# Casting loads for q and k and single-head transposes in a fused attention and gMLP kernel

## The chip, the cores and the metric

The kernel runs on one core of one Trainium2 chip. The metric is the device time of one execution in microseconds (us), lower is better. Most executions of one kernel agree within about 1%. Executions over 1.5% slower than the fastest of the same kernel are left out of the means. The medians below are over all runs, and four of them hold one slow run each; without it they are 174.1 us for e5, 171.1 for e9, 170.16 for e11 and 171.15 for e12. Where a ratio with an interval is given, it is the mean time of one kernel's fast runs over the mean time of the other's fast runs of the same rounds, so it is not quite the ratio of the medians that stand beside it. The interval is the 95% interval.

Engines: PE is the matrix engine (PEld its weight loads), DVE the vector engine, ACT the scalar engine, POOL the GpSimd engine, SP the engine that only issues DMA here. `L266` in a profile line is line 266 of that kernel, so the same step has another line number in each kernel; the text says which step it is.

## The reference, cut to what matters

Attention over 4 batches, 8 heads, 768 positions and 64 dimensions, with a window of 128 and 4 sink positions; then a gated MLP whose gate mixes positions with a 768 x 768 matrix.

```python
scores = scale * q @ k.T                   # 4 x 8 heads, 768 x 768
keep = (pos_k < n_sink) | ((rel >= 0) & (rel < window))
a = softmax(where(keep, scores, -1e9))
x = (a @ v) laid out as [B, S, H * D]      # D = 64, H * D = 512

h = gelu(x @ w_in)                         # 512 -> 1024
u, v = halves of h
v_n = layernorm(v) * g_ln
v_s = einsum('ts,bsd->btd', w_sg, v_n) + b_sg[None, :, None]   # the spatial matmul
out = x + (u * v_s) @ w_out
```

## The kernel before

The kernel is a list of steps, `STEPS`, in one order; each engine executes its own steps in that order and waits, by semaphores, for the data they need. A step is named by what it does, then batch, pair of heads and so on. The names that matter here: LQ, LK, LV load; CQ, CK, CV cast to bf16; TQ, TK transpose on PE; EQ, EK copy the transposes out of PSUM; QK scores, EX exp, MK mask, SK the scores of the sink positions, AV the product with v, NR the division; XD transposes the attention result by DMA; MV and MU are the two halves of the first MLP matmul, SP the spatial matmul, GM the gating product, OU the last projection. `HOLDS` adds waits: "LQ.1.0<LWS" means that this load is issued only when LWS has landed.

```python
# ... (cut: STEPS, 60 lines; it begins)
# IDEN ZERO LC MASK LQ.0.0 LK.0.0 LQ.0.1 LK.0.1 VSK LQ.0.2 LK.0.2 LV.0.0 LQ.0.3 LK.0.3 CQ.0.0 ...
# (and around the DMA transposes of batch 1, which batch 1's MLP waits for)
# ... QK.2.0.1 AV.1.2.0 GM.0.0.2 CQ.2.3 XD.1.1 OU.0.5 ... KS.2.0 XD.1.0 EX.2.1.2 ... LV.3.0 MV.1.2 LQ.3.1 ...
HOLDS = "LQ.1.0<LWS LG<LWS"

def LQ(b, p):                                   # plain fp32 load of one pair of heads, on SP
    return nc.sync.dma_start(out=q32.new((b, p)), in_=q[b, 2 * p:2 * p + 2].rearrange("h (p t) d -> p h (t d)", p=128))

def cast(dst, src):                             # on POOL
    return nc.gpsimd.tensor_scalar(out=dst, in0=src, scalar1=1.0, scalar2=1.0, op0=ALU.mult, op1=ALU.mult)

def CQ(b, p):                                   # interleaves the two heads: [128, NT, 2, 64]
    return cast(q16.new((b, p)).rearrange("p t h d -> p h t d"),
                q32[b, p].rearrange("p h (t d) -> p h t d", d=Dh))
# ... (LK, CK alike)

def transposes(name, ring, b, p):               # six 128 x 128 transposes, two heads in each
    src = ring[b, p].rearrange("p t h d -> p t (h d)")
    mm_ring.new((name, b, p))
    ps = psb((name, b, p))
    for t in range(NT):
        nc.tensor.transpose(ps[:, t, :], src[:, t, :], iden)

def SK(b, p0):                                  # four matmuls accumulate in one 128-row result
    prs = range(HP) if b else (p0,)
    ps = mm_ring.new(("s", b, p0))
    for n, p in enumerate(prs):
        nc.tensor.matmul(ps, ks_sink[b % 2][:, 128 * p:128 * (p + 1)], qT[b, p][:, 256:768],
                         start=(n == 0), stop=(n == len(prs) - 1))

def XD(b, half):                                # transposing DMA, on SP, batches 1 to 3
    ts = slice(3 * half, 3 * half + 3)
    return nc.sync.dma_start_transpose(out=xT.get(b)[:, ts, :, :].rearrange("p t c i -> p (t c) i"),
                                       in_=x_sb[b][:, ts, :].rearrange("p t d -> p (t d)"))
# ... (cut)
```

The softmax here doesn't subtract the row's maximum and nothing guards it: scores larger than these inputs give would overflow.

Of the kernel before, what the change touches and what calls it, by code (L numbers as in the profile page):

```python
# [8 lines left out]
F32 = mybir.dt.float32  # L9
# [6 lines left out]
IDEN ZERO LC MASK LQ.0.0 LK.0.0 LQ.0.1 LK.0.1 VSK LQ.0.2 LK.0.2 LV.0.0 LQ.0.3 LK.0.3 CQ.0.0 LV.0.1 LV.0.2 TQ.0.0  # L16
CK.0.0 VSM.1 LV.0.3 EQ.0.0 TK.0.0 CQ.0.1 EK.0.0 VSM.3 TQ.0.1 CK.0.1 VSM.0 QK.0.0.2 QK.0.0.1 EX.0.0.2 KS.0.0 TK.0.1
EQ.0.1 CQ.0.2 SK.0.0 VSM.2 TQ.0.2 CK.0.2 EQ.0.2 SX.0.0 QK.0.0.0 MK.0.0.2 TK.0.2 EX.0.0.1 CV.0.0 EK.0.2 MK.0.0.1
EX.0.0.0 QK.0.2.2 KS.0.2 CQ.0.3 EX.0.2.2 MK.0.0.0 QK.0.2.0 LW.0 EK.0.1 QK.0.2.1 LW.1 EX.0.2.1 AV.0.0.0 KS.0.1 TQ.0.3
NR.0.0.0 EX.0.2.0 SK.0.1 MK.0.2.2 SK.0.2 MK.0.2.1 AV.0.0.1 SX.0.2 CK.0.3 MK.0.2.0 QK.0.1.0 SX.0.1 QK.0.1.1 CV.0.1  # L20
EX.0.1.0 NR.0.0.1 EQ.0.3 CV.0.2 EX.0.1.1 QK.0.1.2 CV.0.3 MK.0.1.0 TK.0.3 EX.0.1.2 XT.0.0 MK.0.1.1 LWS AV.0.2.1 EK.0.3
AV.0.2.0 XE.0.0 NR.0.2.1 MK.0.1.2 QK.0.3.2 QK.0.3.1 AV.0.1.0 EX.0.3.2 KS.0.3 NR.0.2.0 SK.0.3 LWO AV.0.1.1 EX.0.3.1
NR.0.1.0 QK.0.3.0 MK.0.3.2 XT.0.2 SX.0.3 NR.0.1.1 EX.0.3.0 MK.0.3.1 XT.0.1 XE.0.2 AV.0.3.1 MK.0.3.0 XE.0.1 NR.0.3.1
AV.0.3.0 NR.0.3.0 XT.0.3 XE.0.3 MV.0.2 MU.0.3 GV.0.2 LQ.1.0 LK.1.0 WT.3 WT.4 LV.1.0 WE.3 WT.5 LG WT.2 WE.4 GU.0.3
MV.0.0 WE.5 LQ.1.1 WE.2 LK.1.1 BN.0.2 LV.1.1 MV.0.1 GV.0.0 LQ.1.2 CQ.1.0 LK.1.2 RS.0.2 LV.1.2 BN.0.0 MU.0.0 LQ.1.3
GV.0.1 CK.1.0 LK.1.3 LV.1.3 Z.0.5 WT.1 RS.0.0 LQ.2.0 GU.0.0 TK.1.0 BN.0.1 LK.2.0 MU.0.1 EK.1.0 CV.1.0 Z.0.0 WE.1
TQ.1.0 WT.0 RS.0.1 Z.0.4 Z.0.1 LV.2.0 MU.0.2 WE.0 GU.0.1 EQ.1.0 CQ.1.1 GU.0.2 CK.1.1 Z.0.2 TQ.1.1 LQ.2.1 QK.1.0.2
Z.0.3 QK.1.0.0 LK.2.1 CV.1.1 EX.1.0.2 EQ.1.1 TK.1.1 SP.0.0.3 LV.2.1 CQ.1.2 SP.0.1.2 GT.0.0.3 LQ.2.2 EK.1.1 CK.1.2
GM.0.0.3 SP.0.0.1 EX.1.0.0 GT.0.1.2 MK.1.0.2 LK.2.2 GM.0.1.2 QK.1.1.0 GT.0.0.1 SP.0.1.0 CV.1.2 EX.1.1.0 MK.1.0.0
QK.1.1.1 LV.2.2 GM.0.0.1 CQ.1.3 SP.0.1.1 GT.0.1.0 EX.1.1.1 MK.1.1.0 LQ.2.3 CK.1.3 TQ.1.3 GT.0.1.1 TK.1.2 TQ.1.2  # L30
MK.1.1.1 LK.2.3 EQ.1.3 EK.1.2 TK.1.3 QK.1.0.1 EK.1.3 QK.1.1.2 EQ.1.2 SP.0.0.0 CV.1.3 EX.1.0.1 GM.0.1.1 CQ.2.0 LV.2.3
SP.0.1.3 KS.1.0 EX.1.1.2 MK.1.0.1 LQ.3.0 GT.0.0.0 QK.1.2.1 SK.1.0 GM.0.1.0 EX.1.2.1 GM.0.0.0 MK.1.1.2 GT.0.1.3
QK.1.3.1 SX.1.0 TQ.2.0 GM.0.1.3 MK.1.2.1 QK.1.3.2 EX.1.3.1 EQ.2.0 AV.1.0.0 OU.0.3 NR.1.0.0 CQ.2.1 AV.1.0.1 RA.0.3
MK.1.3.1 TQ.2.1 EX.1.3.2 NR.1.0.1 AV.1.1.1 ST.0.3 QK.1.2.2 CK.2.1 EQ.2.1 QK.1.3.0 EX.1.2.2 AV.1.1.0 OU.0.4 MK.1.3.2
NR.1.1.1 EX.1.3.0 NR.1.1.0 TK.2.1 CQ.2.2 AV.1.3.1 EK.2.1 RA.0.4 QK.1.2.0 CK.2.0 TQ.2.2 NR.1.3.1 EX.1.2.0 ST.0.4
QK.2.1.1 MK.1.2.2 LK.3.0 TK.2.0 EQ.2.2 SP.0.0.2 EX.2.1.1 CK.2.2 MK.1.2.0 EK.2.0 AV.1.2.1 GT.0.0.2 MK.2.1.1 TK.2.2
NR.1.2.1 QK.2.0.2 EK.2.2 QK.2.0.1 AV.1.2.0 GM.0.0.2 CQ.2.3 XD.1.1 OU.0.5 EX.2.0.2 MK.1.3.0 CK.2.3 NR.1.2.0 EX.2.0.1
TQ.2.3 AV.1.3.0 CV.2.2 RA.0.5 TK.2.3 QK.2.1.0 EQ.2.3 MK.2.0.1 EK.2.3 ST.0.5 QK.2.1.2 OU.0.0 EX.2.1.0 NR.1.3.0 CV.2.3
OU.0.2 KS.2.0 XD.1.0 EX.2.1.2 CV.2.1 QK.2.0.0 RA.0.0 SK.2.0 EX.2.0.0 MK.2.1.2 RA.0.2 ST.0.0 OU.0.1 MK.2.1.0 SX.2.0
ST.0.2 CV.2.0 MK.2.0.0 AV.2.1.1 MK.2.0.2 LV.3.0 MV.1.2 LQ.3.1 RA.0.1 CQ.3.0 LK.3.1 NR.2.1.1 ST.0.1 LV.3.1 CK.3.0  # L40
AV.2.0.0 GV.1.2 LQ.3.2 AV.2.1.0 NR.2.0.0 LK.3.2 MV.1.1 LV.3.2 NR.2.1.0 LQ.3.3 LK.3.3 TK.3.0 BN.1.2 LV.3.3 GV.1.1
MV.1.0 EK.3.0 CV.3.0 BN.1.1 MU.1.2 RS.1.2 GV.1.0 CQ.3.1 AV.2.0.1 Z.1.5 GU.1.2 BN.1.0 TQ.3.0 RS.1.1 TQ.3.1 MU.1.0
CK.3.1 Z.1.3 RS.1.0 TK.3.1 EQ.3.1 GU.1.0 MU.1.3 Z.1.4 EK.3.1 NR.2.0.1 CQ.3.2 Z.1.1 MU.1.1 EQ.3.0 CK.3.2 Z.1.0 Z.1.2
TQ.3.2 GU.1.3 CV.3.1 TK.3.2 EQ.3.2 SP.1.1.1 GU.1.1 CV.3.2 EK.3.2 QK.2.2.0 GT.1.1.1 QK.2.3.0 CQ.3.3 SP.1.0.0 EX.2.2.0
GM.1.1.1 CK.3.3 SP.1.1.0 GT.1.0.0 GM.1.0.0 SP.1.0.1 EX.2.3.0 GT.1.1.0 CV.3.3 MK.2.2.0 QK.2.3.1 QK.2.2.2 GM.1.1.0
SP.1.1.3 EX.2.3.1 MK.2.3.0 EX.2.2.2 GT.1.0.1 SP.1.1.2 MK.2.3.1 GT.1.1.3 QK.2.2.1 GM.1.0.1 QK.2.3.2 MK.2.2.2 GM.1.1.3
AV.2.3.0 EX.2.2.1 GT.1.1.2 TQ.3.3 NR.2.3.0 TK.3.3 EX.2.3.2 SP.1.0.2 MK.2.2.1 EQ.3.3 EK.3.3 QK.3.0.1 GT.1.0.2 MK.2.3.2
QK.3.0.2 AV.2.2.0 EX.3.0.1 GM.1.1.2 AV.2.2.1 GM.1.0.2 EX.3.0.2 NR.2.2.0 OU.1.4 MK.3.0.1 NR.2.2.1 XD.2.0 OU.1.5
MK.3.0.2 RA.1.4 QK.3.1.0 RA.1.5 QK.3.0.0 EX.3.1.0 AV.2.3.1 ST.1.4 KS.3.0 ST.1.5 SP.1.0.3 EX.3.0.0 NR.2.3.1 SK.3.0
MK.3.1.0 XD.2.1 GT.1.0.3 QK.3.1.1 SX.3.0 QK.3.1.2 OU.1.3 MK.3.0.0 EX.3.1.2 GM.1.0.3 AV.3.0.0 EX.3.1.1 MK.3.1.2 RA.1.3  # L50
OU.1.2 ST.1.3 MK.3.1.1 OU.1.0 RA.1.2 MV.2.0 ST.1.2 RA.1.0 ST.1.0 MV.2.2 GV.2.0 OU.1.1 GV.2.2 MV.2.1 BN.2.0 BN.2.2
# [16 lines left out]
HOLDS = "LQ.1.0<LWS LG<LWS"  # L68
# [3 lines left out]
def kernel(  # L72
# [14 lines left out]
    nc = tc.nc  # L87
# [14 lines left out]
    NS = n_sink * H  # L102
# [27 lines left out]
    q32 = Ring("q32", 4, [128, 2, NT * Dh], F32)  # L130
    k32 = Ring("k32", 4, [128, 2, NT * Dh], F32)
    v32 = Ring("v32", 4, [128, 2, NT, Dh], F32)
    q16 = Ring("q16", 3, [128, NT, 2, Dh], BF16)
    k16 = Ring("k16", 3, [128, NT, 2, Dh], BF16)
    qT = Ring("qT", 6, [128, S], BF16)
    kT = Ring("kT", 6, [128, S], BF16)
    P = Ring("P", 8, [128, 2, 512], BF16)
# [7 lines left out]
    ot = Ring("ot", 3, [128, d_model], F32)  # L145
    v_sb = [sb.tile([128, H, NT, Dh + 1], BF16, name=f"v_sb{i}") for i in range(2)]
    v_sink = [sb.tile([128, H, Dh + 1], BF16, name=f"v_sink{i}") for i in range(B)]
    ks_w = NS // HP
# [7 lines left out]
    neg_half = sb.tile([128, 2], F32, name="neg_half")  # L156
    vs32 = sb.tile([NS, B, Dh], F32, name="vs32")
# [382 lines left out]
```

## Time and profile before

| | before |
|---|---|
| time, median of 3 runs | 172.4 us (171.82 to 173.63) |
| span of the profiled run | 171.1 us |
| busy PE, DVE, ACT, POOL | 151.1, 138.7, 101.9, 95.9 us |
| first exp, first MLP matmul, first spatial matmul of batch 0 | 11.2, 33.5, 48.9 us |
| first MLP matmul, first spatial matmul of batch 1 | 79.5, 93.2 us |

The two lines below are the head of the page of before, and then its list of the chain that ended last, as shares of the span.

```profile
span 171.1 us, 3623 instructions
...
PE 151.1 (88%) x1388; PEld 90.3 (53%) x1388; DVE 138.7 (81%) x290; ACT 101.9 (60%) x119; POOL 95.9 (56%) x158
...
PE 63%; DVE 20%; ACT 5%; DMA 5%; POOL 3%; issue 2%; DVEq 0%; ACTq 0%
```

PE is busy for 88% of the span and holds 63% of the chain, so time is gained only where PE stands still or does avoidable work. The next lines show where that is: stretches of 10 us with the busy time of PE, PEld, DVE, ACT and POOL (instructions in brackets), the granted PE clock, the DMA share and the GB/s.

```profile
0.00:10.00 10.00, 2.44 (x18) 1.77 (x19) 4.95 (x11) 2.08 (x2) 7.37 (x23) 1.00 0.82 259
10.00:20.00 10.00, 6.98 (x58) 4.12 (x58) 7.72 (x15) 6.62 (x9) 8.72 (x12) 1.00 1.27 250
...
70.00:80.00 10.00, 9.00 (x102) 5.09 (x99) 9.90 (x20) 7.58 (x10) 9.68 (x14) 1.00 0.90 219
80.00:90.00 10.00, 10.00 (x101) 6.35 (x100) 9.64 (x24) 5.05 (x7) 7.80 (x13) 1.00 1.12 306
```

PE does 2.44 us of work in the first 10 us and 6.98 in the next 10; from 80 us on it has no gap until the tail. The head itself, from the timeline of before (start, duration, engine, line, operation, what it makes, count; in brackets the idle time of the engine and what ended it):

```profile
4.74 0.83 POOL L182 TENSOR_SCALAR q<-q 128x768 bf16<-128x768 f32 x1
...
5.63 0.82 PE L266 MATMUL mm<-iden,q 128*128 128x128 bf16 x6 [5.63 <-POOL q L182]
...
7.28 0.80 ACT L281 COPY kT<-mm 128x768 bf16<-128x768 bf16 x1 [1.73 <-PE mm L266]
...
10.63 0.93 PE L310 MATMUL sc<-qT,kT 64*128 64x256 bf16 x8 [1.69 <-DVE qT L276]
...
11.17 0.81 ACT L318 ACTIVATE P<-sc 128x768 bf16<-128x768 f32 x1 [3.09 <-PE sc L310]
```

POOL's cast of the first q pair (L182) releases the first transposes at 5.63 us; the first exp (L318) starts at 11.17 us. Last, the stretch in which batch 1's MLP begins, as the chain of waits shows it (start, length, engine and line):

```profile
77.29 0.97 PE mm L296 x4
...
79.66 1.73 PE sc L399 x8
...
82.12 1.73 PE sc L399 x8
...
85.90 1.30 PE sc L446 x8
```

```profile
DMA to landing us min/median/max: 3.7/4.3/5.0
```

The eight 512-column MLP matmuls of a step (L399) take 1.73 us, and PE goes from one step to the next with small attention work between.

### The profile page before, as it was taken

What the parts mean: (1) busy time and instruction counts of PE and PEld (TensorE: products, weight loads), DVE (VectorE), ACT (ScalarE), POOL (GpSimd) and SP (SyncE); (2) the same over time, 40 slices, a digit from 0 to 9 for tenths busy, and PEclk for the clock granted to TensorE, in tenths of its full rate; (3) what the DMA queues carried; (4) which work ended last, traced back from release to release, by engine and by line L of the source; (5) the groups of instructions that cost most, each with busy time, mean ns of one, the idle gap of its engine ahead of it and who ended that gap; (6) DMA issues with size and microseconds to landing.
All of it is one profiled execution on the core that took longest, in us unless ns stands there. A gap on an engine that the chain in (4) does not pass through costs nothing.

```text
span 171.1 us, 3623 instructions
## 1 busy us (share of the span) xinstructions
PE 151.1 (88%) x1388; PEld 90.3 (53%) x1388; DVE 138.7 (81%) x290; ACT 101.9 (60%) x119; POOL 95.9 (56%) x158
## 2 busy tenths in 40 slices
PE   0447889699989899979999999999999999999970
PEld 0323568364655466645576565544565744556530
DVE  6198696629989999999999799848889994959962
ACT  0416887674995768956649985864997006860000
POOL 7789766013899999999599678043306400520000
PEclk9999999999999999999999999999999999999999
DMA  5999989999999999989999200970100374210044
GB/s 166 325 314 240 210 117 195 221 252 246 316 299 297 279 288 298 314 160 214 321 323 281 64 4 17 230 248 0 61 4 0 64 170 180 80 61 0 34 156 184
DMA packets 49617, 30.94 MB, mean 181 GB/s; under 512 B 35904, under 2 KB 46400, under 8 KB 49600
## 3 DMA queue, kind: packets, MB, share of 16 engines
q1 hardware_dynamic: 47072, 27.93, 61.5%
q0 software_dynamic: 2368, 2.75, 9.8%
q8 instruction: 11, 0.18, 0.4%
q10 hardware_dynamic: 160, 0.03, 0.1%
q14 instruction: 6, 0.05, 0.1%
HBM read 24.81 MB, written 6.29 MB: 182 GB/s over the span
## 4 chain that ended last, share of the span: by engine, by line
PE 63%; DVE 20%; ACT 5%; DMA 5%; POOL 3%; issue 2%; DVEq 0%; ACTq 0%
PE mm L466 15%; PE mm L483 11%; PE sc L446 10%; PE sc L399 10%; PE sc L310 5%; PE mm L266 4%; ACT P L318 3%; DVE qT L276 3%; DVE gtmp L471 3%; PE mm L350 3%; DVE x_sb L370 3%; DMA q<-in_q_dram 3%; DVE P L325 3%; DVE wsg_gated L476 2%; PE mm L356 2%
## 5 line engine op out<-in xcount | busy, mean ns | idle before, releaser
L318 ACT ACTIVATE P<-sc 128x1024 bf16<-128x1024 f32 (+1 forms) x48 | 43.7, 953 | 12.2 <-PE sc L310 10.6
L466 PE MATMUL mm<-wsgT,z 128*128 128x384 bf16 x192 | 34.0, 326 | 0.0
L329 POOL TENSOR_SCALAR_AFFINE_SELECT P<-P 128x512 bf16<-128x512 bf16 x28 | 20.1, 719 | 18.2 <-ACT P L318 13.8
L466 PEld LDWEIGHTS <-z 128*128 128x128 bf16 x192 | 18.0, 98 | 12.1 <-issue 1.2
L483 PE MATMUL mm<-w_out_sb,wsg_gated 128*128 128x512 bf16 x96 | 23.0, 379 | 1.1 <-DVE wsg_gated L476 1.1
L399 PE MATMUL sc<-w_in_sb,xT 128*128 128x512 bf16 x96 | 22.4, 379 | 0.2 <-ACT xT L384 0.2
L446 PE MATMUL sc<-xT,w_in_sb 128*128 128x384 bf16 x128 | 22.4, 326 | 0.0
L471 DVE SCALAR_TENSOR_TENSOR gtmp<-mm,g_sb,b_bc 128x384 bf16<-128x384 f32 x32 | 19.3, 611 | 3.6 <-PE mm L466 3.5
L487 DVE TENSOR_TENSOR ot<-mm,x_sb 128x512 f32<-128x512 f32 x24 | 16.1, 683 | 5.4 <-PE mm L483 5.3
L310 PE MATMUL sc<-qT,kT 64*128 64x256 bf16 x192 | 17.0, 287 | 3.8 <-DVE qT L276 1.7
L350 PE MATMUL mm<-v_sb,P 128*128 128x65 bf16 x192 | 18.0, 201 | 1.6 <-DVE P L325 1.4
L404 ACT ACTIVATE vt<-sc 128x1024 f32<-128x1024 f32 x12 | 12.3, 1024 | 11.7 <-PE sc L399 11.7
L182 POOL TENSOR_SCALAR q<-q 128x768 bf16<-128x768 f32 x16 | 14.3, 891 | 8.6 <-DMA q<-in_q_dram 8.6
L370 DVE TENSOR_TENSOR x_sb<-mm,rcp 128x384 bf16<-128x384 f32 x32 | 17.8, 557 | 1.1
L350 PEld LDWEIGHTS <-P 128*128 128x128 bf16 x192 | 15.2, 102 | 5.9 <-issue 2.1
L411 DVE BATCH_NORM_STATS2 st<-vt 128x6 f32<-128x512 f32 x24 | 16.2, 675 | 2.5 <-ACT vt L404 2.5
L325 DVE TENSOR_TENSOR P<-P,mask 128x1024 bf16<-128x1024 bf16 x20 | 16.4, 830 | 1.3 <-ACT P L318 1.1
L356 PE MATMUL mm<-v_sb,P 128*128 128x65 bf16 x160 | 16.9, 200 | 0.0
L446 PEld LDWEIGHTS <-w_in_sb 128*128 128x128 bf16 x128 | 12.4, 98 | 8.4
L281 ACT COPY kT<-mm 128x768 bf16<-128x768 bf16 x16 | 12.8, 801 | 5.6 <-PE mm L266 5.6
L182 POOL TENSOR_SCALAR v_sb<-v 128x768 bf16<-128x768 f32 x16 | 14.9, 937 | 1.9 <-DMA v<-in_v_dram 1.9
L418 POOL TENSOR_SCALAR rs<-mv 128x2 f32<-128x2 f32 x12 | 3.0, 251 | 22.6 <-DVE mv L412 22.2
(61 smaller groups left out, 253.8 us busy)
## 6 DMA issues: line engine op xcount, KB each, us to landing
q<-in_q_dram SPq DMA_DIRECT2D x16, 384.0 KB, 6.6
k<-in_k_dram SPq DMA_DIRECT2D x16, 384.0 KB, 5.8
v<-in_v_dram SPq DMA_DIRECT2D x16, 384.0 KB, 6.9
out_dram<-ot SPq DMA_DIRECT2D x24, 256.0 KB, 2.0
wsg_gated<-in_moe_w_sg_dram POOLq DMA_DIRECT2D x1, 1152.0 KB, 8.8
w_in_sb<-in_moe_w_in_dram POOLq DMA_DIRECT2D x2, 512.0 KB, 7.2
w_out_sb<-in_moe_w_out_dram POOLq DMA_DIRECT2D x1, 512.0 KB, 8.1
b_bc<-in_moe_b_sg_dram SPq DMA_DIRECT2D x1, 384.0 KB
```

Of the source, the lines that this page charges most:

```text
L182: return nc.gpsimd.tensor_scalar(out=dst, in0=src, scalar1=1.0, scalar2=1.0, op0=ALU.mult, op1=ALU.mult)
L310: nc.tensor.matmul(sc[:, hl, 256 * jl:256 * jl + n], kT[b, p][rows, 128 * j:128 * (j + 1)], qT[b, p][rows, 128 * j:128 * j + n], start=Tru ...
L318: nc.scalar.activation(out=pt[:, :, 0:w], in_=sc_ring[b, p, g][:, :, 0:w], func=AF.Exp, scale=scale)
L325: nc.vector.tensor_mul(pt[:, :, 0:w], pt[:, :, 0:w], m.unsqueeze(1).to_broadcast([128, 2, w]))
L350: nc.tensor.matmul(av[:, il, hl, :], P[b, p, i // 2][:, hl, 256 * (i % 2):256 * (i % 2) + 128], vb[:, h, i, :], start=first, stop=False)
L356: nc.tensor.matmul(av[:, il, hl, :], P[b, p, j // 2][:, hl, 256 * (j % 2) + 128:256 * (j % 2) + 256], vb[:, h, j, :], start=False, stop=False)
L370: nc.vector.tensor_mul(xs[:, 3 * half:3 * half + 3, 128 * p:128 * (p + 1)].rearrange("p t (h d) -> p t h d", h=2), av[:, :, :, 0:Dh], rcp. ...
L399: nc.tensor.matmul(hp[:, jl, :], xT[b][:, j, c, :], w_in_sb[:, c, d_half:2 * d_half], start=(c == 0), stop=(c == KD - 1))
L446: nc.tensor.matmul(hp[:, hf, 0:NH], w_in_sb[:, c, 128 * dc:128 * (dc + 1)], xT[b][:, 3 * hf:3 * hf + 3, c, :], start=(c == 0), stop=(c == ...
L466: nc.tensor.matmul(ps[:, 0:NH], z[b][:, si, 128 * dc:128 * (dc + 1)], wsgT[:, si, NH * hf:NH * (hf + 1)], start=(si == 0), stop=(si == NT ...
L471: nc.vector.scalar_tensor_tensor(out=gtmp.new((b, hf, dc)), in0=mm_ring["g", b, hf, dc][:, 0:NH], scalar=g_sb[:, dc:dc + 1], in1=b_bc[:, N ...
L483: nc.tensor.matmul(ps, gatedT[:, (2 * b + hf) % 3, dc, 128 * tl:128 * (tl + 1)], w_out_sb[:, dc, :], start=(dc == 0), stop=(dc == KU - 1))
```

## The change

Its intent: take the 32 casts of q and k off POOL by letting the DMA cast on the way (such loads are issued by POOL, four heads in one from batch 1 on, two in batch 0); as those loads leave the heads side by side rather than interleaved, each head is transposed by itself, two transposes in the two column halves of the array. The first pair of q and k still comes by plain loads with casts on ACT. The sink scores use four 32-column tiles instead of four accumulating matmuls. POOL, relieved, takes over some gating products, and DVE takes over masks. The weights' first load waits for LV.0.1. The order of all steps is new. The core of the diff:

```diff
-IDEN ZERO LC MASK LQ.0.0 LK.0.0 LQ.0.1 LK.0.1 VSK LQ.0.2 LK.0.2 LV.0.0 LQ.0.3 LK.0.3 CQ.0.0 LV.0.1 LV.0.2 TQ.0.0
+LQ.0.0 LQ.0.1 FILL LK.0.0 LK.0.1 LV.0.0 ZERO LV.0.1 LQ.0.2 LC MASK IDEN CQ.0.0.A MASK0 LK.0.2 LQ.0.3 TQ.0.0 LV.0.2
+TQ.0.1 LK.0.3 EQ.0.0.A EQ.0.1.A VSK TK.0.1 EK.0.1.A TQ.0.2 CK.0.0.A KS.0.1 QK.0.1.1 EQ.0.2.D SK.0.1 EX.0.1.1 QK.0.1.2
 ... (cut; around the DMA transposes of batch 1)
+AV.1.3.0 SP.0.0.0 NR.1.3.1 EX.2.1.2 MK.1.2.2.P NR.1.3.0 QK.2.1.0 CV.2.2.A QK.2.1.1 OU.0.3 GT.0.0.0 XD.1.0 EX.2.1.1
+KS.2.0 AV.1.2.1 EX.2.1.0 GM.0.0.0.P RA.0.3 TQ.2.0 NR.1.2.1 TQ.2.2 ST.0.3 EQ.2.0.A MK.2.1.1.P OU.0.2 EQ.2.2.D XD.1.1
+CV.2.3.A LQ.3.0 QK.2.0.2 QK.2.0.1 MK.2.1.0 EX.2.0.2 OU.0.1 LK.3.0 MK.2.1.2.D EX.2.0.1 QK.2.0.0 MK.2.0.2.D LQ.3.1
+SK.2.0 RA.0.1 OU.0.0 EX.2.0.0 LK.3.1 CV.2.1.D ST.0.1 SX.2.0 MV.1.0 MK.2.0.1.P RA.0.2 LV.3.1 CV.3.0.A RA.0.0 LV.3.2
 ... (cut)
-HOLDS = "LQ.1.0<LWS LG<LWS"
+HOLDS = "LW.0<LV.0.1 LV.1.0<LWS LG<LWS"
-    q16 = Ring("q16", 3, [128, NT, 2, Dh], BF16)
+    q16 = Ring("q16", 2, [128, 4, NT, Dh], BF16)
+    def load(ring, src, b, i):                     # casting load, issued by POOL
+        n = 2 if b == 0 else 4
+        hs = slice(n * i, n * i + n)
+        dst = ring.get((b, n * i // 4))[:, n * i % 4:n * i % 4 + n].rearrange("p h t d -> p h (t d)")
+        return nc.gpsimd.dma_start(out=dst, in_=src[b, hs].rearrange("h (p t) d -> p h (t d)", p=128))
     def transposes(name, ring, b, p):
         for t in range(NT):
-            nc.tensor.transpose(ps[:, t, :], src[:, t, :], iden)
+            for hl in range(2):
+                nc.tensor.transpose(ps[64 * hl:64 * hl + 64, t, :], src[:, 2 * (p % 2) + hl, t, :], iden)
     def SK(b, p0):
-        for n, p in enumerate(prs):
-            nc.tensor.matmul(ps, ks_sink[b % 2][:, 128 * p:128 * (p + 1)], qT[b, p][:, 256:768],
-                             start=(n == 0), stop=(n == len(prs) - 1))
+        for p in range(HP):                        # (batch 0 keeps one matmul for each pair)
+            c0 = (128 + ks_w) * p
+            nc.tensor.matmul(ps[ks_w * p:ks_w * (p + 1), :], ks[:, c0:c0 + ks_w], qT[b, p][:, 256:768],
+                             start=True, stop=True)
-    def GM(b, hf, dc):
-        nc.vector.tensor_mul(gatedT[:, (2 * b + hf) % 3, dc, :], gtmp[b, hf, dc],
+    def GM(b, hf, dc, e):
+        (nc.vector if e == "D" else nc.gpsimd).tensor_mul(gatedT[:, (2 * b + hf) % 3, dc, :], gtmp[b, hf, dc],
                              uT[b][:, dc, NH * hf:NH * (hf + 1)])
```

## The prediction

> **What bounds the kernel now.** The list of busy times gives PE 151.1 of 171.1 us (88%), DVE 138.7, ACT 101.9, POOL 95.9. From 80 us on the windows table shows PE busy without a break until the tail; in the chain of waits PE lines hold 63%. Spacing the matmuls as the timeline shows them when dense (128 columns 56 ns, 384 columns 162, 512 columns 216, a row-paired score matmul about 55[...]) PE needs about 143 us. So 28 us are lost, by 10-us windows: 9 in 0-10, 7 in 10-20, 3 in 20-30, 2 in 30-40, 3 in 40-80, and 5 in the tail. The head is the prize. There POOL casts each q and k pair (0.83 us or more, in one queue with v casts and masks); the first transpose starts at 5.63 us, the first exp at 11.17, the first MLP matmul of batch 0 at 34.5, the first spatial (wsgT) matmul at 48.9. In 50-74 us the chain runs on DVE, which is 98% busy.
>
> **What changes.**
> - Head: 32 POOL casts go (28.6 us), 18 casting DMA issues come (about 0.87 us each, as the weight issues show: 16 us). The second pair needs no cast, so the first exp should come at 8 to 8.5 us. The rest of batch 0 is then bound by ACT: 23 us of work (12 exps 11.4, 4 sink exps 2.4, copies 8, table 1.3). First MLP matmul at about 30 us: 4 to 5 us earlier. Weights are issued back to back, not between POOL work (before: 15.5, 23.2, 26.5 us). Summed packet times put the last q/k of batch 1 at about 45 us, which caps what is kept at the first spatial matmul at 3 to 4 us.
> - Sink scores of batches 1-3: four accumulating 512-column matmuls (0.97 us in the chain) become four 32-column tiles that should overlap: 0.7 us x3 = 2 us of PE saved.
> - Transposes: 192 become 384, two single-head ones beside each other. The Trainium skill, "TensorEngine Tiling (Array Packing)", Key Properties, says that different tiles execute weight loads and matmuls in parallel, but that a change of mode drains the array. The trace shows pairing for row tiles alone: score pairs start 4 ns apart, about 110 ns a pair. I expect 12 transposes in 0.40 to 0.45 us against 0.34: 2 to 3 us lost over batches 1-3.
> - DVE: loses 20 gating products (0.48 us each) and 5 net evictions (0.95), gains 10 mask products (0.65-0.83), 5 v casts and small ones: about -2 us. ACT +8, POOL -30; neither binds after 40 us.
> - Tail: all spatial matmuls precede the last six projections; the 1.0 us wait before the last three goes.
>
> Sum: -3.5 -2 +2.5 -1, -2 for less DVE/POOL pressure in 50-80 us: about -6 us.
>
> **Prediction: 166.0 us, 161.5 to 170.0 eight times in ten. Faster by over 2%: 0.77; within 2%: 0.18; slower: 0.05.**
>
> **What would show it.** First exp before 9 us; first MLP matmul near 30; first spatial matmul near 45.5; POOL's waits for q loads gone; transposes 56-75 ns per pair; sink matmuls of a batch 0.25-0.3 us; PE unbroken from 46 us on.
>
> **What would make it wrong.** Single-head transposes not overlapping (0.67 us for 12: 8 us lost, result near 171). Batch 1's casting loads late, so PE waits before the spatial matmuls. Gating products slow on POOL, delaying projections. Or a better head (near 160).

## More of the kernel before

For two of the six transposing DMAs, both of later batches, the trace gives the landing: 3.7 and 5.0 us after the issue. No matmul waits long for any of them (PE's waits list none).

## The result, and the profile after

The changed kernel is correct and slower: 182.23 us median of 4 runs (181.08 to 183.35) against 172.2 us of before (171.82 to 173.63, 4 runs). The ratio is 1.0566 (1.0475 to 1.0657).

The head of the page after, and the chain's shares:

```profile
span 181.6 us, 3949 instructions
...
PE 154.7 (85%) x1580; PEld 89.7 (49%) x1580; DVE 136.2 (75%) x303; ACT 108.9 (60%) x129; POOL 74.0 (41%) x102
...
PE 69%; DMA 13%; DVE 12%; ACT 2%; issue 2%; POOL 1%; DVEq 1%; POOLq 0%
```

PE's busy time grew by only 3.6 us; the span grew by 10.5. The chain now has 13% under DMA, where it had 5%. The stretches of 5 us around batch 1's MLP, in the same columns as before's stretches, show where:

```profile
75.00:80.00 5.00, 4.30 (x38) 1.49 (x32) 4.96 (x9) 4.93 (x7) 4.97 (x7) 1.00 1.10 139
80.00:85.00 5.00, 4.38 (x53) 2.55 (x53) 3.13 (x9) 2.76 (x3) 0.01 (x1) 1.00 1.26 212
85.00:90.00 5.00, 0.00 (x0) 0.00 (x0) 1.80 (x5) 0.00 (x0) 0.00 (x0) 0.96 1.35 161
90.00:95.00 5.00, 3.62 (x9) 1.35 (x10) 0.63 (x1) 1.02 (x1) 0.00 (x0) 0.50 1.25 272
```

From 85 to 90 us PE does nothing at all, and POOL and ACT nothing either, while the DMA share is 1.35. In 90 to 95 us PE works, but at a granted clock of 0.50. The chain of waits through the same stretch names the cause:

```profile
76.70 0.29 PE mm L505
77.00 14.34 DMA xT<-x_sb
...
91.38 5.24 PE sc L428 x12
96.62 1.30 PE sc L468 x8
```

The piece at 77.00 us is the second transposing DMA of batch 1 (XD.1.1). It holds the chain for 14.34 us. The twelve MLP matmuls behind it (L428) then take 5.24 us; at the spacing before, 1.73 us for eight, they would take 2.6. So the slow clock cost about 2.6 us on top of the wait. The query of the tile xT, and the list of what PE waited for:

```profile
DMA to landing us min/median/max: 3.6/3.6/14.3
```

```profile
PE sc L428 <- DMA xT<-x_sb: 7.6, 2, 6.7
```

Of the six transposing DMAs the trace gives the landing of five. Their median is 3.6 us. One takes 14.3, and PE waits 6.7 us for it at one go. (The view counts only DMAs whose landing is known, so it says nothing of XD.1.0 here, nor in e1, e2 and e10.)

The head also moved, the wrong way. Its timeline (ACT L207 the casts and copies, PE L294 the transposes, L344 the scores, ACT L352 exp):

```profile
4.09 0.83 ACT L207 CAST q<-v 128x768 bf16<-128x768 f32 x1 [2.02 <-DMA v<-in_q_dram]
...
5.15 0.85 PE L294 MATMUL mm<-iden,q 128*64 128x128 bf16 x12 [5.15 <-POOL iden masks.py:199]
...
7.84 0.85 PE L294 MATMUL mm<-iden,q 128*64 128x128 bf16 x12 [1.84 <-DMA q<-in_q_dram]
...
10.13 0.85 PE L294 MATMUL mm<-iden,k 128*64 128x128 bf16 x12 [1.44 <-DMA k<-in_k_dram]
...
11.71 0.83 ACT L207 CAST k<-v 128x768 bf16<-128x768 f32 x1
...
12.34 0.61 PE L344 MATMUL sc<-qT,kT 64*128 64x256 bf16 x4
...
12.99 1.78 ACT L352 ACTIVATE P<-sc 128x1024 bf16<-128x1024 f32 x2 [0.44 <-PE sc L344]
```

The first exp comes at 12.99 us, not at 11.17 as before, and not at 8 to 8.5 as predicted. The transposes wait first for the identity matrix (built on POOL behind the masks), then for the casting load of the second q pair (until 7.84 us) and of the second k pair (until 10.13). The first k pair was on the chip early, issued at 1.31 us by a plain load like the q whose cast starts at 4.09, but ACT reaches its cast only at 11.71, behind copies that wait for the casting loads.

Milestones of the two profiled runs, in us from the start:

| | first exp | MLP b0 | spatial b0 | MLP b1 | second half (MU) of MLP b1 | spatial b1 | end |
|---|---|---|---|---|---|---|---|
| before | 11.2 | 33.5 | 48.9 | 79.5 | 85.7 | 93.2 | 171.1 |
| after | 13.0 | 35.5 | 52.1 | 80.2 | 96.5 | 103.6 | 181.6 |

The 10.5 us of these two profiles add up so: 3.2 lost up to the first spatial matmul; 2.5 gained from there to batch 1's first MLP matmul (30.6 us before, 28.1 after); 10.1 lost between the two halves of that MLP (6.2 us before, 16.3 after); about 0.3 gained in all the rest. The head's share is uncertain by more than a microsecond: after's profile is that of its slowest run, and e1, e2, e3 and e10, whose head has the same order, reach the first spatial matmul at 50.2 to 51.3 us; e7 and e8, whose order is that of before, at 48.7. The head's loss is thus between 1.3 and 3.4 us.

### The profile page after: what moved, and what is told of

Same layout as the page of the kernel before. It is cut to its first block, busy times and chain, and to the rows that moved or that the text cites. A ratio compares the mean times of both kernels' runs of the same rounds, so it can differ in the third digit from the quotient of the medians.

```text
span 181.6 us, 3949 instructions
## 1 busy us (share of the span) xinstructions
PE 154.7 (85%) x1580; PEld 89.7 (49%) x1580; DVE 136.2 (75%) x303; ACT 108.9 (60%) x129; POOL 74.0 (41%) x102
## 4 chain that ended last, share of the span: by engine, by line
PE 69%; DMA 13%; DVE 12%; ACT 2%; issue 2%; POOL 1%; DVEq 1%; POOLq 0%
PE mm L488 14%; PE sc L468 12%; PE sc L428 11%; PE mm L505 11%; DMA xT<-x_sb 8%; PE mm L294 6%; PE sc L344 6%; DMA q<-in_q_dram 5%; DVE P L359 4%; PE mm L384 3%; PE mm L390 2%; DVE gtmp L493 2%; ACT P L352 2%; PE mm L394 2%; DVE x_sb L404 1%
## 5 line engine op out<-in xcount | busy, mean ns | idle before, releaser
L352 ACT ACTIVATE P<-sc 128x1024 bf16<-128x1024 f32 (+1 forms) x48 | 43.8, 955 | 7.8 <-PE sc L344 7.6
L488 PE MATMUL mm<-wsgT,z 128*128 128x384 bf16 x192 | 34.6, 327 | 0.0
L428 PE MATMUL sc<-w_in_sb,xT 128*128 128x512 bf16 x96 | 25.0, 410 | 7.8 <-DMA xT<-x_sb 7.6
L432 ACT ACTIVATE vt<-sc 128x1024 f32<-128x1024 f32 x12 | 12.3, 1023 | 30.8 <-PE sc L428 30.8
L498 POOL TENSOR_TENSOR wsg_gated<-gtmp,uT 128x384 bf16<-128x384 bf16 x20 | 20.1, 1014 | 24.4 <-DVE gtmp L493 24.3
L449 POOL TENSOR_TENSOR rs<-rs,neg_half 128x4 f32<-128x4 f32 (+1 forms) x8 | 7.2, 895 | 49.8 <-DVE rs L444 43.0
L363 POOL TENSOR_SCALAR_AFFINE_SELECT P<-P 128x512 bf16<-128x512 bf16 x18 | 13.6, 753 | 22.7 <-ACT P L352 22.7
L359 DVE TENSOR_TENSOR P<-P,mask 128x1024 bf16<-128x1024 bf16 (+1 forms) x30 | 21.2, 727 | 0.4 <-ACT P L352 0.2
L344 PE MATMUL sc<-qT,kT 64*128 64x256 bf16 x192 | 17.8, 291 | 3.5 <-ACT P L352 2.0
L428 PEld LDWEIGHTS <-xT 128*128 128x128 bf16 x96 | 9.6, 104 | 20.6 <-DMA xT<-x_sb 8.6
L384 PE MATMUL mm<-v_sb,P 128*128 128x65 bf16 x192 | 17.6, 201 | 1.3 <-DVE P L359 1.2
L384 PEld LDWEIGHTS <-P 128*128 128x128 bf16 x192 | 15.2, 102 | 5.4 <-DVE P L359 2.0
L473 ACT ACTIVATE uT<-sc 128x768 bf16<-128x768 f32 x16 | 12.9, 807 | 6.2 <-PE sc L468 6.2
L390 PE MATMUL mm<-v_sb,P 128*128 128x65 bf16 x160 | 16.5, 200 | 0.0
```

The source lines that it names most:

```text
L344: nc.tensor.matmul(sc[:, hl, 256 * jl:256 * jl + n], kT[b, p][rows, 128 * j:128 * (j + 1)], qT[b, p][rows, 128 * j:128 * j + n], start=Tru ...
L352: nc.scalar.activation(out=pt[:, :, 0:w], in_=sc_ring[b, p, g][:, :, 0:w], func=AF.Exp, scale=scale)
L359: nc.vector.tensor_mul(pt[:, :, 0:w], pt[:, :, 0:w], m.unsqueeze(1).to_broadcast([128, 2, w]))
L384: nc.tensor.matmul(av[:, il, hl, :], P[b, p, i // 2][:, hl, 256 * (i % 2):256 * (i % 2) + 128], vb[:, h, i, :], start=first, stop=False)
L390: nc.tensor.matmul(av[:, il, hl, :], P[b, p, j // 2][:, hl, 256 * (j % 2) + 128:256 * (j % 2) + 256], vb[:, h, j, :], start=False, stop=False)
L428: nc.tensor.matmul(hp[:, jl, :], xT[b][:, j, c, :], w_in_sb[:, c, d_half:2 * d_half], start=(c == 0), stop=(c == KD - 1))
```

## The experiments

The theories. The main one, for the stall: the four casting loads of batch 3, issued by POOL from 75.4 to 78.4 us into their own queue, run beside XD.1.1, and each DMA engine takes the two queues' packets in turn. A casting load's packet (768 bytes at its destination) occupies an engine 2.6 times as long as one of the transposing DMA (256 bytes) in the stretch counted below (80.1 ns against 30.6), so the transposing DMA gets a small share of the engines. Its rival: these are simply many bytes at the time of the DMA, in whatever form and queue. For the head: the order in which the first pairs are cast makes batch 0 late, or, the rival, a better order makes the first exp early and the end no earlier, as the later pairs wait for their loads anyhow (C and D, where a recorded expectation uses letters for them). The packet records of the trace support the turn by packets. They are counted here for 82 to 88 us of after:

```text
queue   bytes   packets   mean ns   engine time, mean of 16 engines, us
0 (POOL, casting)       768   1100   80.1   5.51
1 (SP, transposing)     256   1126   30.6   2.16
```

(Packets overlap in an engine, so the two times add up to more than the 6 us.) One for one, as taking turns would have it. The Trainium skill, "DMA: Bandwidth & Descriptors", section "Queues, rings and completion order", says so: each engine "round-robins between the queue rows it has work for, at *packet* granularity". The records agree with 1100 against 1126; the page adds that such a packet is typically some 9 to 17 descriptors, and the counts cannot show whether the records come in such groups. The page does not say what follows for queues of unequal packets: the queue of small ones got 28% of the engine time here (2.16 of 7.67). The same records split the 14.3 us: XD.1.1's 1536 packets start 4.6 us after its issue, with another store's packets and casting loads running before them, and then take 9.2 us (81.6 to 90.8). In e1 below, without casting loads beside it, the same 1536 start 1.3 us after the issue and take 2.1 us.

### e1: batch 3's first casting load held until XD.1.1 has landed

```diff
-HOLDS = "LW.0<LV.0.1 LV.1.0<LWS LG<LWS"
+HOLDS = "LW.0<LV.0.1 LV.1.0<LWS LG<LWS LQ.3.0<XD.1.1"
```

> One wait added to the changed kernel: the casting loads of batch 3 (q and k, 4 x 768 KB of float32) are issued by POOL only when the second transposing DMA of batch 1 has landed. Theory A (the 14 us that this transposing DMA took to land, and the PE idle time at 84-91 us, come from sharing the DMA engines with the four casting loads issued at 75.4-78.4 us): it lands in 4 to 5 us, its waits at the second MLP matmul group of batch 1 fall from 7.6 us to under 1 us, the granted clock stays above 0.95 in 80-100 us, and the time falls by 5 to 9 us to 173-177; not all of it, since POOL, blocked until the landing, makes later masks and loads of batch 3 late. Rival B (the transposing DMA is held up on its own queue, by the stores and v loads around it, or by its late issue): landing stays over 10 us and the time stays within 1 us of 182.

Measured: 178.37 us, ratio 1.0325 (1.0295 to 1.0356). What the tile xT shows, and the second entry of PE's waits:

```profile
DMA to landing us min/median/max: 3.6/3.6/3.9
```

```profile
PE mm L384 <- POOL P L363: 4.2, 1, 4.2
```

XD.1.1 lands in 3.9 us, so the casting loads are what held it up. The time missed the expected 173 to 177 us and the clock the expected 0.95: the gain was 3.9 us and not more, because a held load holds everything behind it on POOL. POOL's masks come late and PE waits 4.2 us for one, and the clock falls again (0.53 in 85 to 90 us). The cause is confirmed, the hold is a poor remedy.

### e2: all four casting loads of batch 3 issued early

Four buffers instead of two let the loads go right behind batch 2's.

```diff
-... EK.1.2.D CV.1.1.P LK.2.1 LV.2.1 QK.1.1.0 ...    (LQ.3.0 LK.3.0 LQ.3.1 LK.3.1 behind XD.1.1)
+... EK.1.2.D CV.1.1.P LK.2.1 LQ.3.0 LK.3.0 LQ.3.1 LK.3.1 LV.2.1 QK.1.1.0 ...
-    q16 = Ring("q16", 2, [128, 4, NT, Dh], BF16)    (k16 alike)
+    q16 = Ring("q16", 4, [128, 4, NT, Dh], BF16)
```

> The casting loads of batch 3 are issued about 22 us earlier (right after those of batch 2, into rings of four buffers instead of two), so that they run at 60-70 us, where the changed kernel leaves the DMA engines half idle. Theory A: both transposing DMAs of batch 1 land in 4 to 5 us, no PE wait on them over 1 us, PE not idle over 3 us there, and 9 to 11 us go: 171 to 173 us. Rival B: the transposing DMA stays at 10 us or more and the time within 1 us of 182.

Measured: 174.85 us, ratio 1.0141 (1.0082 to 1.0199).

```profile
DMA to landing us min/median/max: 3.6/3.7/3.9
```

This takes back 7.4 of the 10 us by moving four load issues. What stays is 2.1 us over before, some 2 us more than expected. The stretch and PE's waits show a second, smaller stall just before batch 1's MLP:

```profile
75.00:80.00 5.00, 2.74 (x16) 0.93 (x16) 2.77 (x5) 4.52 (x6) 1.58 (x3) 0.77 1.11 222
```

```profile
PE sc L344 <- ACT qT L207: 2.0, 1, 2.0
```

ACT idles 2.5 us for a load of v (its cast starts at 73.80 us), its copy of q comes late, PE waits 2.0 us for that at 77.21, and the clock is 0.50 from 77.7 to 81.2 us.

### e3: the same bytes by plain loads, in the same queue as XD.1.1

Batch 3's q and k come in fp32 by SP, issued right behind XD.1.1, and POOL casts them. This was meant to tell the turn by packets from the mere bytes: the same bytes are read and the loads are issued at about the same time, but behind the DMA in its own queue, not beside it in another.

```diff
+    def plain3(name, src, i):
+        return nc.sync.dma_start(out=n32.new((name, i)).rearrange("p h t d -> p h (t d)"), in_=...)
-... XD.1.1 CV.2.3.A LQ.3.0 QK.2.0.2 ... LK.3.0 ... LQ.3.1 ... LK.3.1 ...
+... XD.1.1 LQ.3.0 LK.3.0 LQ.3.1 LK.3.1 CV.2.3.A QK.2.0.2 ... C3.0.1 TQ.3.3 ...      (C3: the casts, on POOL)
```

> Batch 3's q and k are loaded without a cast by the SP queue, issued right behind the second transposing DMA of batch 1 (the same bytes read, the same moment, about twice the bytes written), and cast by POOL. Theory A in its sharp form (two queues are served packet by packet in turn, so a queue of 256-byte packets next to one of 768-byte packets that take four times as long gets about a fifth of the engines; in one queue the order of issue holds): the transposing DMA lands in 4 to 5 us although the same bytes are moving, and the PE wait goes; 172 to 176 us. Theory A in its blunt form (it is the bytes in flight): it lands in 10 us or more and little is gained. The stores and v loads behind those loads come later, which may cost 1 to 3 us.

Measured: 177.61 us, ratio 1.0287 (1.0265 to 1.0309). The tile xT, and the stretch 90 to 95 us:

```profile
DMA to landing us min/median/max: 3.8/3.8/3.8
```

```profile
90.00:95.00 5.00, 2.83 (x53) 1.98 (x54) 5.00 (x5) 2.65 (x4) 5.00 (x5) 0.96 1.22 263
```

The trace gives one landing, that of XD.1.1: 3.8 us. So these loads do no harm from behind, in the same queue. The run doesn't refute the rival, though: the packet records have the plain loads' first packet at 79.3 us and XD.1.1's last at 79.4; only 59 of their 2048 packets start before it lands. The bytes moved after the DMA, not with it. What speaks for turns by packets is the count in after's own records; no run put packets of equal size, or a queue of small ones, beside XD.1.1. The time, expected at 172 to 176 us, was missed. The time lost moved to 90 to 95 us, where POOL is busy for all 5.00 us with the casts that this experiment brought back, and PE for 2.83.

### e4: the order of the first pairs

Otherwise as after: pair 0 first, its k cast right behind its q, and the identity before the masks.

```diff
-... LV.0.1 LQ.0.2 LC MASK IDEN CQ.0.0.A MASK0 LK.0.2 LQ.0.3 TQ.0.0 LV.0.2 TQ.0.1 ...
+... LV.0.1 IDEN LQ.0.2 LC MASK CQ.0.0.A CK.0.0.A MASK0 LK.0.2 LQ.0.3 TQ.0.0 LV.0.2 EQ.0.0.A TK.0.0 ...
```

> Only batch 0's order is changed: the pair that comes by plain loads (pair 0) is cast, transposed and scored first, its k cast right behind its q cast on ACT, and the identity is built before the masks. Theory C (the head is late because ACT and PE wait in order for the casting loads of pairs 1 and 2 while the plain k lies there from about 5.5 us): first exp at 8.5 to 9.5 us instead of 13.0, first MLP matmul of batch 0 at 31.5 to 33.5 instead of 35.5, and 2 to 4 us less in all: 178 to 180 us. Rival D (the head is bound by the arrival of all of q and k, shared with v and the weights): first exp earlier, but the first MLP matmul stays at 35 or later, time within 1 us of 182.

Measured: 181.57 us, ratio 1.0525 (1.0494 to 1.0557).

```profile
8.46 1.79 ACT L352 ACTIVATE P<-sc 128x1024 bf16<-128x1024 f32 x2 [1.84 <-PE sc L344]
```

The first exp comes at 8.46 us, where the prediction had it, but from the pair with plain loads, not from the second pair as the prediction had it. The first MLP matmul of batch 0 comes at 34.2 us, within the 33.7 to 35.5 of after, e1, e2, e3 and e10, whose head has the old order, and the time differs from after's by 0.7 us, with overlapping intervals. An early first exp is not an early batch 0; that the later pairs' loads hold it back, as the rival has it, fits but is not shown. The stall at XD.1.1 is still there (15.2 us to landing), so this run cannot tell what a better head would be worth without it.

### e5: e2, e4's order, and the sink rows of v loaded and built earlier

```diff
-LQ.0.0 LQ.0.1 FILL LK.0.0 LK.0.1 LV.0.0 ZERO LV.0.1 LQ.0.2 LC MASK IDEN ...
+LQ.0.0 LQ.0.1 FILL LK.0.0 LK.0.1 LC LV.0.0 ZERO LV.0.1 IDEN LQ.0.2 MASK VSK ...      (VSM.0 to VSM.3 also earlier)
```

> The kernel with the early batch-3 loads (174.85 us), plus batch 0 in the order of the swapped-head run, plus the four small sink-row loads of v issued before the v loads and the four sink-v builds on DVE done at 8-13 us, where DVE idles, instead of at 19-35 us. Theory E (after the first exp the head is bound by DVE, which does 0.85 us of sink-v building four times inside its chain at 19-35 us because those rows come behind two v loads on the SP queue): first exp at 8.5 us, first MLP matmul of batch 0 at 30.5 to 32.5 us, 2.5 to 4 us less: 171 to 172.5 us. Rival D (the head is bound by the arrival of the q, k loads): first MLP matmul no earlier than 33.5 us and at most 1 us gained.

Measured: 174.73 us (174.1 on the fast runs), ratio 1.0113 (1.0063 to 1.0164), no different from e2's 174.85 and 1.0141 (1.0082 to 1.0199). In its profile the first MLP matmul comes at 32.2 us and the first spatial at 48.6, 2.4 and 2.6 us earlier than in e2, but batch 1's MLP only at 84.1. That profile fell on a slow run (177.66 us), so what it shows of the middle is a lead and no proof:

```profile
72.34 1.57 ACT L207 CAST v_sb<-v 128x768 bf16<-128x768 f32 x2 [7.77 <-DMA v<-in_v_dram]
```

ACT idles 7.77 us for a load of v; in e2's profile, of a fast run, it is the 2.5 us named above. Up to there the casting loads run without a break beside v's loads, which also have 256-byte packets (for 52 to 68 us of this profile the records count 2966 packets of 768 bytes, 78.2 ns each, and 2911 of 256 bytes, 30.8 ns each: again one for one). That made the next question: whether the head is worth something once batch 3's casting loads do not run beside v's loads either.

### e6: e2 with batch 3's first v load behind XD.1.1

```diff
-AV.1.3.1 NR.1.2.0 LV.3.0 EX.1.2.2 ... XD.1.1 CV.2.3.A ...
+AV.1.3.1 NR.1.2.0 EX.1.2.2 ... XD.1.1 LV.3.0 CV.2.3.A ...      (its cast moved to POOL, next to CV.3.1)
```

> The kernel with the early batch-3 loads, with the first v load of batch 3 issued behind the transposing DMAs of batch 1 instead of before them, and its cast moved from ACT to POOL beside the next pairs' casts. Theory A says that what is left of the stall at 75-80 us (PE 2.7 of 5 us busy, granted clock 0.77) is the same sharing again, in one queue: the first transposing DMA stands behind two v loads of about 2 us each. So the first transposing DMA lands about 2 us earlier, PE idles less, and 1 to 3 us go: 172 to 174 us. If the stall comes from ACT or DVE work (the q and k evictions that PE waits for), nothing changes (within 0.7 us).

Measured: 175.86 us, ratio 1.0189 (1.0134 to 1.0245). Nothing was gained over e2, so this load is not where e2's remaining 2 us lie. The other branch of the expectation, a stall from ACT's copies, fits its trace: PE waits 2.7 us for ACT's copy of q, and ACT had waited 3.1 us for another load of v.

### e7: before, with the four sink matmuls side by side

```diff
-        for n, p in enumerate(prs):
-            nc.tensor.matmul(ps, ks_sink[b % 2][:, 128 * p:128 * (p + 1)], qT[b, p][:, 256:768],
-                             start=(n == 0), stop=(n == len(prs) - 1))
+        for p in range(HP):
+            c0 = (128 + ks_w) * p
+            nc.tensor.matmul(ps[ks_w * p:ks_w * (p + 1), :], ks[:, c0:c0 + ks_w], qT[b, p][:, 256:768],
+                             start=True, stop=True)      (batch 0 as it was; sink rows laid out 16 to a head)
```

> The kernel before with one part of the change alone: the sink scores of batches 1 to 3 as four 32-column matmuls beside each other. If they overlap and PE is the bound, PE loses 3 x 0.75 us of work and the time falls by 1 to 2.3 us; four of them take 0.2 to 0.3 us of PE in place of 0.97. If they do not overlap: time within 0.5 us of before.

Measured: 172.2 us, ratio 0.9991 (0.9952 to 1.003). Batch 2's sink matmuls in the timelines, first of before, then of e7:

```profile
77.23 1.04 PE L296 MATMUL mm<-qT,ks_sink 128*128 128x512 bf16 x4
```

```profile
77.05 0.40 PE L298 MATMUL mm<-qT,ks_sink 128*32 128x512 bf16 x4
```

Four matmuls end 0.40 us after the first begins, against 1.04; they start within 10 ns. The Trainium skill, "TensorE: Matmul & The Clock Gate", Part 3, gives about 4 ns for each further tile; this trace agrees. Yet the time doesn't move, where 1 to 2.3 us were expected. Two of the three places are at about 59 and 77 us, where DVE is busy for about 98% of the time (9.90 of 10 us in 70 to 80). At 59 us the chain of before lies on DVE. At 77 us it lies on PE, but only just: in e7 the chain from 74.4 to 78.2 us is DVE's, then ACT's exp of the sinks, for which PE waits 0.27 us, and batch 1's MLP starts at 79.24 us instead of 79.50. The end of the span moved by 0.6 us, about what the third place saves, which is within the scatter.

### e8: before, with single-head transposes

POOL still casts, but leaves the heads side by side.

```diff
-    q16 = Ring("q16", 3, [128, NT, 2, Dh], BF16)
+    q16 = Ring("q16", 3, [128, 2, NT, Dh], BF16)
         for t in range(NT):
-            nc.tensor.transpose(ps[:, t, :], src[:, t, :], iden)
+            for hl in range(2):
+                nc.tensor.transpose(ps[64 * hl:64 * hl + 64, t, :], src[:, hl, t, :], iden)
```

> The kernel before with one part of the change alone: the POOL casts write head by head, and two single-head transposes stand where one of both heads stood. The changed kernel's trace has 12 of them in 0.33-0.34 us where dense, so they overlap in full: time within 0.7 us of before. The prediction had assumed 0.40 to 0.45 us for 12, which would be 2 to 3 us slower. POOL's casts write contiguous runs of 768 elements instead of 64, which may make them a little faster.

Measured: 174.87 us, ratio 1.0139 (1.0086 to 1.0191): about 2 us lost, where at most 0.7 was expected. The transposes between two MLP steps, first in before, then in e8:

```profile
88.25 1.46 PE L446 MATMUL sc<-xT,w_in_sb 128*128 128x384 bf16 x8
89.55 0.50 PE L266 MATMUL mm<-iden,k 128*128 128x128 bf16 x6
89.88 2.76 PE L446 MATMUL sc<-xT,w_in_sb 128*128 128x384 bf16 x16
```

```profile
88.84 1.48 PE L447 MATMUL sc<-xT,w_in_sb 128*128 128x384 bf16 x8
90.25 0.53 PE L267 MATMUL mm<-iden,k 128*64 128x128 bf16 x12
90.70 2.77 PE L447 MATMUL sc<-xT,w_in_sb 128*128 128x384 bf16 x16
```

From the start of one MLP group to the start of the next it is 1.63 us before and 1.86 us here. The transposes themselves overlap nearly as hoped: 12 take 306 ns from first start to last, 6 double ones 279. Most of the loss lies at the edges, where the array goes from full width to half width and back: last matmul to first transpose 256 ns instead of 163, last transpose to next matmul 151 instead of 56. In all 0.22 us for each visit, whether it has 12 transposes (714 ns between two MLP matmuls instead of 498) or 24 (1049 instead of 833). Beside score matmuls, which use half the rows and so change the mode in both kernels, nothing is lost (201 against 199 ns). The Trainium skill, "TensorEngine Tiling (Array Packing)", Key Properties, says that a change of tiling mode drains the array; it gives no figure, and these are the figures. The page also says under Restrictions that column tiling turns off Fast Weight Load; within such a row its cost can be no more than the 27 ns by which 306 exceeds 279.

### e9 and e10: the casting loads in two groups, with and without e5's head

Four buffers, as in e2, but LQ.3.1 and LK.3.1 go behind GM.0.1.0 and the other two behind MK.2.0.1 with a hold on XD.1.1, to keep them off v's loads and the transposing DMA. e9 has e5's head, e10 the head of after.

```diff
-HOLDS = "LW.0<LV.0.1 LV.1.0<LWS LG<LWS"
+HOLDS = "LW.0<LV.0.1 LV.1.0<LWS LG<LWS LQ.3.0<XD.1.1"
+... GM.0.1.0.P LQ.3.1 LK.3.1 QK.1.2.1 ... MV.1.0 MK.2.0.1.P LQ.3.0 LK.3.0 RA.0.2 LV.3.1 ...
```

> The changed kernel with batch 0 in the swapped order, the sink rows of v loaded and built early, and the casting loads of batch 3 split: those of heads 4-7 issued at about 62 us, behind the casting loads of batch 2, those of heads 0-3 held until the second transposing DMA of batch 1 has landed. In the run with all of them early (e5) the casting queue ran without a break from 45 to 70 us, and the v loads next to it, in packets of 256 bytes, got one packet for one of the others: they took 8 us each, and ACT waited 7.8 us for one. Theory A for both: with the split, the v loads of batch 2 and both transposing DMAs keep to their times (first MLP matmul of batch 1 at 77 to 79 us, no PE or ACT wait over 2 us on a load there), the head gain of e5 (first spatial matmul at 48.6 us) is kept, and the time is 170 to 173.5 us. If something else takes the head gain back, it stays at 174.5 us or more.

> The changed kernel with the split of batch 3's casting loads alone (head as changed). Theory A: the stall at 80-91 us goes as in e2: 174 to 176 us; and e9 minus e10 is what the head order is worth once nothing takes it back: 2 to 3 us (first spatial matmul 51 us here, 48.6 there).

Measured: e9 171.73 us, ratio 0.9899 (0.9807 to 0.999); e10 175.09 us, ratio 1.0132 (1.0055 to 1.0209). (The transposing DMAs land within 6.9 us in e9's profile, which is that of its slow run, and within 3.9 in e10's, for the five of six that it gives.) The two differ in the head alone, by 3.4 us, or 4.0 with e9's fast runs, and the intervals don't touch. So a better head is real time that is kept to the end once nothing in the middle takes it back. It is the order and the early sink rows together: no run tells them apart without the stall. In the milestones of the profiles the two heads are closer, 50.2 us in e10 to the first spatial matmul against 49.1 in e9 and 47.8 in e12, the same kernel.

### e11 and e12: one casting load early and three held; and e9 again

```diff
-... GM.0.1.0.P LQ.3.1 LK.3.1 QK.1.2.1 ... MK.2.0.1.P LQ.3.0 LK.3.0 RA.0.2 ...
+... GM.0.1.0.P LQ.3.1 QK.1.2.1 ... MK.2.0.1.P LQ.3.0 LK.3.0 LK.3.1 RA.0.2 ...      (e11)
```

> As the split-and-head run, with only one casting load of batch 3 (q of heads 4-7) before the transposing DMAs of batch 1 and the other three behind the second one. If the first transposing DMA still lost time to the two early loads in the split-and-head run (its issue took 5.3 us there against 1.4 to 1.9 in the kernel before), it is issued in under 4 us now and up to 1.5 us more go: 170 to 171.5 us. If the three late loads come too late for batch 3's transposes, PE waits for them at 88-95 us and the time is 172 us or more.

> The split-and-head kernel again, with more rounds: its four runs spread from 170.2 to 173.0 us. If it beats the kernel before, the ratio is 0.985 to 0.995 with the whole interval below 1; if the first reading was luck, the interval holds 1.

Measured, five rounds on one chip, before 172.58 us: e11 170.36 us, ratio 0.9857 (0.9805 to 0.991); e12, which is e9 unchanged, 171.44 us, ratio 0.9916 (0.9859 to 0.9974). e11 beats both kernels, before by 1.4% and after by about 12 us. e11 is what the change gives once its loads are placed and its head is put right. By the milestones of the profiles e11's gain over before doesn't come from the head, whose first spatial matmul is at 48.9 us in both: it comes from there to batch 1's MLP (26.9 us against 30.6), and 1.4 us of it are lost again later.

The runs side by side (medians; milestones from the profile of each, in us):

| kernel | time | first exp | MLP b0 | spatial b0 | MLP b1 | MU b1 |
|---|---|---|---|---|---|---|
| before | 172.2 | 11.2 | 33.5 | 48.9 | 79.5 | 85.7 |
| after | 182.23 | 13.0 | 35.5 | 52.1 | 80.2 | 96.5 |
| e1 hold | 178.37 | 12.5 | 33.7 | 50.3 | 77.5 | 91.4 |
| e2 early | 174.85 | 12.8 | 34.6 | 51.2 | 81.7 | 88.3 |
| e4 head alone | 181.57 | 8.5 | 34.2 | 50.7 | 79.2 | 95.5 |
| e10 two groups | 175.09 | 12.5 | 33.7 | 50.2 | 78.9 | 85.5 |
| e11 two groups, head | 170.36 | 8.5 | 32.5 | 48.9 | 75.8 | 82.4 |

## Why the prediction was wrong

It said 166.0 us, within 161.5 to 170.0, and 0.77 for faster; it was 182.23. Point by point:

- **Missing: the stall, about +10 us.** This is the step that failed most: "PE unbroken from 46 us on", where the runs show PE idle for 6.7 us at a transposing DMA. The sum "-3.5 -2 +2.5 -1, -2" has no term for a DMA that lands late. The prediction named late casting loads as a risk, "Batch 1's casting loads late, so PE waits before the spatial matmuls". Those were not late; it was batch 3's that came in the way of batch 1's transposing DMA. e1, e2 and e3 show the cause, each by an edit of its own that takes the casting loads away from beside XD.1.1: its landing time goes from 14.3 to under 4 us. The wait was 6.7 us at one go, and the rest is mostly the halved clock after it (the twelve matmuls: 5.24 us against 2.6). The Trainium skill, "TensorE: Matmul & The Clock Gate", Part 1, tells of half the clock after an idle window of about 3.4 us; this trace agrees, with 0.50 from 89.6 us, 5 us into the idle time, to 96.4. Idle need not mean one long wait: in e2 the clock went to 0.50 at 77.7 us after 3.4 us in which PE was busy for 1.36 and waited for no more than 2.0 at a time. The order of the steps had the needed fact: LQ.3.0 to LK.3.1 stand right behind XD.1.1. But the stall alone does not explain the miss: without it, e2 and e10 still took 174.9 and 175.1 us, above before and above the prediction's range.
- **The head: -3.5 us expected, +3.2 in the profile of after (1.3 to 3.4 with the scatter named above).** "The second pair needs no cast, so the first exp should come at 8 to 8.5 us" took for granted that this pair's loads are there early. Even the plain loads of before were not: POOL's casts of the second q and k start at 7.24 and 8.35 us, on waiting for them. In the trace of after, the second q pair's load was issued at 1.30 us and released its transposes at 7.84, the second k pair's, issued at 2.25, at 10.13; and as PE and ACT keep to their order, the first pair, which had landed, waited behind them. e4 shows that the order alone sets the first exp (8.46 us); e10 against e9 shows that order and sink rows together were worth 3.4 us. "First MLP matmul at about 30 us" was never reached; the best was 31.4 (e12), and the first spatial matmul came at 47.8 us at best, against 48.9 in before and the predicted 45.5. (The prediction's own starting point, 34.5 us for the first MLP matmul, was 1 us late: the trace has 33.5.)
- **The transposes: 2 to 3 us expected, about 2.1 measured (e8).** The size was right by luck, for the reason was another: 12 were to take 0.40 to 0.45 us against 0.34, but they take hardly longer (306 ns against 279 from first start to last). Each visit between full-width matmuls pays about 0.22 us, of which 0.19 fall at its two edges. The prediction had named the drain at a change of mode, but did not count it by visits.
- **The sink matmuls: "0.7 us x3 = 2 us of PE saved", about 0 measured (e7).** They overlap as said, and PE's work falls by 0.6 us each time. But two of three lie where DVE is as late as PE or later, which the prediction itself had written down ("In 50-74 us the chain runs on DVE"), without drawing on it here.
- **DVE "-2 us", ACT "+8", POOL "-30".** DVE fell from 138.7 to 136.2 and ACT rose from 101.9 to 108.9, as predicted. POOL fell from 95.9 to 74.0, by 22 and not 30; a gating product takes 1.01 us on POOL against 0.48 on DVE, so 20 of them are 20.1 us, and the prediction doesn't say what it counted for them. POOL holds only 1% of the chain after.
- **"-2 for less DVE/POOL pressure in 50-80 us".** From the first spatial matmul to batch 1's MLP the changed kernel needed 28.1 us against 30.6. So the size of this term was right, at -2.5; what in that stretch earned it was not tested, as transposes and sink matmuls fall there too.
- **Tail.** The wait before the last projections went from 1.1 us to 0, as said.
- **The lost time.** "PE needs about 143 us" rested on a spacing of 52 ns for the 65-column matmuls: in the trace of before their median is 29 to 30 ns. With 30 the sum is about 135 us (an estimate from the same counts and spacings), so more time was lost than the prediction thought.

The sum corrected, from the two profiles: +10.1 for the stall, +3.2 for the head, -2.5 for 50 to 80 us, about -0.3 in the rest. What stays open: how much of e11's and e9's remaining time is the transposes' 2 us, as no kernel was run with casting loads and double transposes (these loads leave the heads side by side); and what in e5 took the head's gain back, as its profile fell on a slow run (the wait for v's loads, which e2's fast profile shows too, is the likely cause, not a shown one). Open too is whether it takes packets of unequal size to slow a transposing DMA so. What makes e11 faster than e9 (170.36 against 171.44, with overlapping intervals) isn't settled either.

## What to carry to other kernels

When a change moves loads to another DMA queue, look up what every small, urgent transfer will run beside; here a queue of larger packets next to it made a 4 us transfer take 14. Moving those loads in the order of issue is the cheap remedy, as long as nothing urgent stands behind a held one; look up what they run beside in their new place too. When engines keep to a fixed order, put first what lands first, and judge the head by the first large stage that it feeds, not by its first instruction. Price small array tiles by the number of visits between full-width matmuls, and count a saving on one engine only where that engine sets the pace.

## What the Trainium skill lacked or had wrong

- "DMA: Bandwidth & Descriptors", "Queues, rings and completion order": it tells of the turn by packets, but not of the result for queues of unequal packets. Here 1100 packets of 768 bytes went with 1126 of 256 bytes, and a transposing DMA took 14.3 us from issue to landing, against 3.8 to 3.9 for the same one in e1, e2 and e3. In the same page's "Rules for kernel authors", "A transpose next to ordinary DMAs needs nothing" holds for its result (all runs were correct), but not for its time.
- "TensorEngine Tiling (Array Packing)", "Key Properties": the drain at a change of mode has no figure. Here it is 0.09 us on entering and 0.1 us on leaving, and with 0.03 us more for the transposes themselves 0.22 us in all, for each visit of half-width transposes between full-width matmuls, and nothing beside matmuls that are tiled already.
- "TensorE: Matmul & The Clock Gate", "Part 4": it gives about 275 to 390 ns for one transpose. Here one takes 242 ns on average, and in a dense row they start 56 ns apart, which is what counts in a sum.
